# Key copies of the even blocks moved behind the second mask, and half of the first two conversions of v moved from GpSimd to ScalarE

## The chip, the cores and the metric

The kernel runs on one core of one Trainium2 chip. The metric is the time of one execution on the device in microseconds (us). "TensorE", "VectorE", "ScalarE" and "GpSimd" are PE, DVE, ACT and POOL in the profile; SP issues the transfers.

The unchanged kernel scatters: 44 executions of it in this study ran from 184.82 to 189.39 us, with a median of 186.8. A run counts as slow when it is over 1.5% above the fastest run of the same kernel, and the verdicts leave such runs out. No separate slow state of the core is visible here; the scatter is a band, and its causes are part of this story.

## The reference, cut to what matters

Attention over 8 batches, 8 heads, 576 positions and a head size of 64, followed by a gated layer on the joined heads:

```python
mask_plain = (rel >= 0) & (rel < 32)                        # heads 0 to 3
mask_dil = (rel >= 0) & (rel < 128) & (rel % 4 == 0)        # heads 4 to 7
attn = softmax(where(mask, scale * q @ k.T, -1e9));  x = attn @ v
gate = sigmoid(causal depthwise convolution of x over 5 positions, conv_w)
out = (gate * (x @ w_val)) @ w_out
```

## The kernel before

The work is cut into 32 steps, two heads each; four steps make a batch: two plain pairs, then two dilated pairs. I number steps from 0, so steps 2 and 3 are the first dilated ones. Two pairs of one kind in one batch form a group (group 0 plain, group 1 dilated, group 2 plain of the next batch, and so on). Each step does the scores of its own pair on TensorE, the exponentials on ScalarE, the masks on VectorE, the product with v on TensorE, and the transposes of the keys and queries that the next group needs. For plain heads a second copy of the keys is made, kE, in which the even blocks of 96 keys stand next to the keys that a window reaches into. It is copied from kT by VectorE, where the transposes are read out:

```python
else:                                   # the keys of a plain group
    t["kT"] = kTs[(g // 2) % NKT]
    nc.scalar.copy(                     # ScalarE: transposed keys from PSUM to kT
        out=t["kT"][:, z0:z1, 0:RM].rearrange("p z (t r) -> p z t r", r=DIL),
        in_=src.rearrange("p z (r t) -> p z t r", r=DIL))
    ke = t["kE"] = kEs[(g // 2) % NKT]
    kt = t["kT"][:, z0:z1, :].rearrange("p z (u s) -> p z u s", u=NB // 2)
    nc.vector.tensor_copy(ke[:, z0:z1, :, 0:96], kt[:, :, :, 0:96])
    nc.vector.tensor_copy(
        ke[:, z0:z1, 1:NB // 2, 96:128], kt[:, :, 0:NB // 2 - 1, 160:192])
```

The order of a step from number 7 on (earlier steps have a form of their own, marked by `i < EARLY`):

```python
scores(i, 0); scores(i, 1)
run_conv(i - 1)
apply_mask(i, 0)
after_x(i - 1)                                     # reads out xT
if g + 1 < 2 * B:
    trans_main(g + 1, "k" if a == 0 else "q")      # holds the code above
apply_mask(i, 1)
...
attn_v(i, 0); attn_v(i, 1)
normalize(i)
if (a == 0 or i == EARLY) and g + 1 < 2 * B:
    trans_rest(g + 1)                              # the last 64 positions
...                                                # output and value products
```

v of the plain heads comes in as float32 and is converted by four copies on GpSimd, the last two of which the change concerns:

```python
nc.gpsimd.tensor_copy(x[32:64, :, 2:NB, :], w[64:96, :, 0:NB - 2, :])
nc.gpsimd.tensor_copy(x[0:48], w[0:48])
nc.gpsimd.tensor_copy(x[64:96], w[32:64])
nc.gpsimd.tensor_copy(x[96:128], w[64:96])
```

Of the kernel before, what the change touches and what calls it, by code (L numbers as in the profile page):

```python
# [23 lines left out]
def kernel(  # L24
# [11 lines left out]
    nc = tc.nc  # L36

    B, H, S, D = q.shape
# [10 lines left out]
    NB = 6  # L49
# [32 lines left out]
    NKT = 2  # L82
    kTs = [consts.tile([128, 2, S], BF16, name=f"kT{i}") for i in range(NKT)]

    kEs = [consts.tile([128, 2, NB // 2, 128], BF16, name=f"kE{i}") for i in range(NKT)]
    NET = 2
    ets = [consts.tile([128, 2, 2 * HB + 96], BF16, name=f"et{i}") for i in range(NET)]
    NVP = 2
    vPst = [consts.tile([96, 4, NB // 2, 2 * D], FP32, name=f"vPst{i}") for i in range(NVP)]
    vPs = [consts.tile([128, 4, NB, 66], BF16, name=f"vP{i}") for i in range(NVP)]  # L90
# [21 lines left out]
    def bank_b():  # L112
        return bank().bitcast(BF16).rearrange("p (z n) -> p z n", z=2)


    grp_tiles = {}
# [68 lines left out]
    def prep_v(i):  # L185
        b, c, dil, g, a = pair_info(i)
        t = grp_tiles[g]
        e = a + 2
        if not dil:


            w = vPst[b % NVP][:, a:e].rearrange("p h u (j d) -> p h (u j) d", j=2)
            x = vPs[b % NVP][:, a:e, :, 0:D]
            nc.gpsimd.tensor_copy(x[32:64, :, 2:NB, :], w[64:96, :, 0:NB - 2, :])
            nc.gpsimd.tensor_copy(x[0:48], w[0:48])  # L195
            nc.gpsimd.tensor_copy(x[64:96], w[32:64])  # L196
            nc.gpsimd.tensor_copy(x[96:128], w[64:96])  # L197
        else:
            nc.gpsimd.tensor_copy(
                vAs[b % NVD][:, a:e, :, 0:D],  # L200
                t["vst"][:, a:e, :].rearrange("p h (r d) -> p h r d", r=DIL))
            nc.gpsimd.tensor_copy(
                vBs[b % NVD][:, a:e, :, 0:D], t["vBst"][:, a:e, :, :])

    def pair_info(i):
        b, c = i // NCH, i % NCH
        dil = int(c >= NCH // 2)
        return b, c, dil, 2 * b + dil, (c % 2) * 2

    def load_pair(g, a):  # L210
# [26 lines left out]
        out=ident, in_=ident, compare_op=ALU.not_equal, fill=1.0,  # L237
# [5 lines left out]
        out=ident5, in_=ident5, compare_op=ALU.not_equal, fill=1.0,  # L243
# [28 lines left out]
    for j in range(2):  # L272
        for (z, dst) in ((0, mask_p[:, 2 + j, :]), (1, mtmp)):
            band(dst.rearrange("p (r t) -> p r t", r=4), [[1, 4], [4, 24]], 160 * z - j, 2)
        nc.gpsimd.tensor_tensor(
            out=mask_p[:, 2 + j, :], in0=mask_p[:, 2 + j, :], in1=mtmp, op=ALU.add)
# [3 lines left out]
        out=mh, in_=mh, compare_op=ALU.is_ge, fill=1.0,  # L280
# [74 lines left out]
    def trans_main(g, name, pairs=(0, 1)):  # L355

        dil = g % 2
        t = grp_tiles[g]
        ps = bank_b()
        for z in pairs:  # L360
            for m in range(4):
                if not dil and g < 6:
                    for h in range(2):
                        nc.tensor.transpose(
                            out=ps[D * h:D * h + D, z, TM * m:TM * m + TM],
                            in_=hi_bf16(t[name][:, 2 * z + h, D * m:D * m + D]), identity=ident)
                    continue
                elif not dil:
                    src = t[name + "b"][:, m, 2 * z:2 * z + 2, :]
                else:  # L370
                    src = hi_bf16(t[name][:, 2 * z + m // 2, 128 * (m % 2):128 * (m % 2) + 128])
                nc.tensor.transpose(out=ps[:, z, TM * m:TM * m + TM], in_=src, identity=ident)  # L372
        z0, z1 = pairs[0], pairs[-1] + 1
        src = ps[:, z0:z1, :]
        rt = src.rearrange("p z (r t) -> p z r t", r=DIL)
        if not dil:
            if name == "q":
                if "qT" not in t:
                    t["qT"] = qt_pool.tile([128, 2, DIL, T], BF16, name="qT")
                dst = t["qT"][:, z0:z1, :, 0:TM]  # L380
                if g == 0 and z0 == 0:
                    nc.vector.tensor_copy(dst, rt)
                else:
                    nc.scalar.copy(out=dst, in_=rt)
            else:
                t["kT"] = kTs[(g // 2) % NKT]
                nc.scalar.copy(  # L387
                    out=t["kT"][:, z0:z1, 0:RM].rearrange("p z (t r) -> p z t r", r=DIL),
                    in_=src.rearrange("p z (r t) -> p z t r", r=DIL))
                ke = t["kE"] = kEs[(g // 2) % NKT]  # L390
                kt = t["kT"][:, z0:z1, :].rearrange("p z (u s) -> p z u s", u=NB // 2)
                nc.vector.tensor_copy(ke[:, z0:z1, :, 0:96], kt[:, :, :, 0:96])
                nc.vector.tensor_copy(
                    ke[:, z0:z1, 1:NB // 2, 96:128], kt[:, :, 0:NB // 2 - 1, 160:192])
        else:
            A = name + "A"
            if A not in t:
                t[A] = qt_pool.tile([128, 2, RM], BF16, name=A)
            nc.scalar.copy(out=t[A][:, z0:z1, :], in_=src)
            if name == "k":  # L400
                if "kB" not in t:
                    t["kB"] = qt_pool.tile([128, 4, 64, 2], BF16, name="kB")
                nc.scalar.copy(  # L403
                    out=t["kB"][:, 2 * z0:2 * z1, 0:TM - TB, :],
                    in_=src.rearrange("p z (h w t) -> p (z h) t w", h=2, w=2)[:, :, TB:TM, :])

    def trans_rest(g):
        dil = g % 2
# [260 lines left out]
    def warm(n):  # L669
        for _ in range(n):  # L670
            nc.tensor.matmul(out=bank(), lhsT=junk[:, 0:128], rhs=junk, start=True, stop=True)
# [11 lines left out]

    def early_rest(i):

        if i == 0:
            setup_conv_w()
            make_conv_diag(0)
            warm(3)
        run_conv(i - 1)  # L690
        apply_mask(i, 0)
        if i == 0:
            make_conv_diag(1)
        if i > 0:
            after_x(i - 1)
        apply_mask(i, 1)
        if i == 0:
            make_conv_diag(2)
            next_pair(i, ("k",))
        elif i < NCH:  # L700
            next_pair(i)
        if i < NCH:
            warm(2)
        else:
            run_val()
        attn_v(i, 0)
        attn_v(i, 1)
        if i == 0:
            next_pair(i, ("q",))
        normalize(i)  # L710
        if i == 0:
            make_conv_diag(3)
        if i < NCH:
            warm(1)
        else:
            run_val()
            next_pair(i)
        if i == 5:
            run_val()
            run_val()  # L720
        elif i == 6:
            run_out()
            trans_main(4, "k")
            run_out()
# [10 lines left out]
    for i in range(NP):  # L735
        b, c, dil, g, a = pair_info(i)

        if i == 0:
            load_weight(0, moe_w_val)
            load_pair(2, 0)  # L740
        elif i == 1:
            load_pair(2, 2)
        elif i == 2:
            load_weight(1, moe_w_out)
            load_pair(3, 0)
        elif i == 3:
            load_pair(3, 2)
            load_group(4)
        if c % 2 == 0 and 5 <= g + 3 < 2 * B:
            load_group(g + 3)  # L750

        if i == 0:
            prep_v(0)
            make_mask_d()
            prep_v(1)
            make_perm()
        elif i < 3:
            prep_v(i + 1)
        elif i == 3:
            cast_val()  # L760
            prep_v(4)
            swap_val()
        elif i == 4:
            prep_v(5)
            cast_out()
            prep_v(6)
        elif i == 5:
            prep_v(7)
        elif i == 6:
            for m in range(NCH):  # L770
                for h in range(2):
                    swap_out(h, m)
        elif i > 6:
            if i < NP - 1:
                prep_v(i + 1)
            if g + 2 < 2 * B and g % 2 == 0:
                cast(g + 2, "k" if a == 0 else "q")
        scores(i, 0)
        scores(i, 1)
        if i < EARLY:  # L780
            early_rest(i)
            continue
        run_conv(i - 1)
        apply_mask(i, 0)
        after_x(i - 1)
        if g + 1 < 2 * B:
            trans_main(g + 1, "k" if a == 0 else "q")
        apply_mask(i, 1)
        if c == 0 and outs:
            run_out()  # L790
        elif vals:
            run_val()
        attn_v(i, 0)
        attn_v(i, 1)
        normalize(i)
        if (a == 0 or i == EARLY) and g + 1 < 2 * B:
            trans_rest(g + 1)
        if c == 0 and vals:
            run_val()
        for _ in range((2 if len(outs) > 2 else 1) - (c == 0 and i > NCH)):  # L800
            if outs:
                run_out()
        if vals:
            run_val()
# [39 lines left out]
```

## Time and profile before

| | before |
|---|---|
| three timings before the prediction | 186.5, 188.51, 189.39 us |
| span of the profiled execution | 186.8 us |
| TensorE busy | 160.9 us |
| VectorE, ScalarE, GpSimd busy | 133.7, 114.1, 102.6 us |

The page's first part (busy time, share of the span, instructions) and the row of GpSimd in its second part (busy tenths in 40 slices of 4.67 us):

```profile
PE 160.9 (86%) x2850; PEld 107.9 (58%) x2875; DVE 133.7 (72%) x320; ACT 114.1 (61%) x215; POOL 102.6 (55%) x177
POOL 7789949999999758902892268508963000000000
```

TensorE is the engine that is fullest, so the kernel is shortened by taking away its pauses. GpSimd is near full from about 10 to 60 us and takes turns afterwards. While it works, the same VectorE instruction can take longer: the second of the two key copies takes 0.17 us in step 10 of this profile and 0.82 us in step 7, where GpSimd converts v beside it. The prediction quotes the waits and the timeline on which it rests.

### The profile page before, as it was taken

How to read it: one execution, taken by the hardware profiler on the slowest of the kernel's cores; microseconds unless marked ns; L12 is line 12 of the kernel's file. 1: busy time of each engine (PE TensorE's matmuls, PEld its weight loads, DVE VectorE, ACT ScalarE, POOL GpSimd, SP SyncE). 2: the span in 40 equal slices, each digit the busy share in tenths (PEclk: the TensorE clock that was granted, in tenths of full speed). 3: DMA queues.
4: the chain of work that ended last, by engine and by line, in shares of the span. 5: the costliest groups of instructions: out<-in, count | busy, mean ns of one | idle time of the engine just before them, and what ended most of it. 6: DMA issues, size and time to landing. Idle time of an engine off the chain costs nothing.

```text
span 186.8 us, 6930 instructions
## 1 busy us (share of the span) xinstructions
PE 160.9 (86%) x2850; PEld 107.9 (58%) x2875; DVE 133.7 (72%) x320; ACT 114.1 (61%) x215; POOL 102.6 (55%) x177
## 2 busy tenths in 40 slices
PE   6785898788899699989999799979997899999990
PEld 2343565465567476756676466656675667665540
DVE  5594899777769687968876787877696877784320
ACT  3324663646886677776777477657867587654441
POOL 7789949999999758902892268508963000000000
PEclk9879699999999999999999999999999999999998
DMA  5999999999999995959889888879487122222355
GB/s 143 245 299 344 261 233 341 304 273 308 334 270 329 361 228 171 334 164 278 199 278 282 240 232 263 263 243 306 130 261 241 54 65 60 61 57 77 97 168 168
DMA packets 48298, 41.88 MB, mean 224 GB/s; under 512 B 6789, under 2 KB 42629, under 8 KB 48266
## 3 DMA queue, kind: packets, MB, share of 16 engines
q1 hardware_dynamic: 47712, 41.10, 78.3%
q8 instruction: 22, 0.36, 0.9%
q10 hardware_dynamic: 554, 0.34, 0.6%
q14 instruction: 10, 0.08, 0.2%
HBM read 31.99 MB, written 9.44 MB: 222 GB/s over the span
## 4 chain that ended last, share of the span: by engine, by line
PE 55%; DVE 21%; ACT 9%; POOL 6%; issue 4%; DMA 3%; SPq 1%; POOLq 0%; ACTq 0%
PE ps_bank L629 15%; PE ps_bank L612 12%; DVE et L479 9%; PE ps_bank L595 8%; PE ps_bank L372 3%; PE ps_sc L500 3%; DMA vPst<-in_v_dram 3%; ACT kT L387 3%; ACT et L470 3%; PE ps_sc L514 3%; DVE xT L564 3%; PE ps_sc L450 3%; PE ps_sc L467 2%; DVE xn L530 2%; DVE xn L537 2%
## 5 line engine op out<-in xcount | busy, mean ns | idle before, releaser
L470 ACT ACTIVATE et<-ps_sc 128x576 bf16<-128x576 f32 x64 | 38.2, 648 | 18.0 <-PE ps_sc L450 9.5
L634 ACT ACTIVATE osb<-ps_bank 128x512 f32<-128x512 f32 x36 | 21.9, 609 | 34.1 <-PE ps_bank L629 27.5
L618 DVE SCALAR_TENSOR_TENSOR y<-gate,ps_bank 128x288 bf16<-128x288 bf16 x64 | 28.2, 448 | 9.6 <-PE ps_bank L612 8.1
L595 PE MATMUL ps_bank<-xT,conv_diag 64*64 64x288 bf16 (+1 forms) x768 | 27.9, 270 | 0.0
L530 DVE TENSOR_TENSOR xn<-ps_sc,rec 128x768 bf16<-128x768 f32 (+1 forms) x27 | 25.8, 956 | 0.9
L479 DVE TENSOR_TENSOR et<-et,mask_d 128x576 bf16<-128x576 bf16 x32 | 20.9, 653 | 5.1 <-ACT et L470 4.9
L604 ACT ACTIVATE gate<-ps_bank 128x288 bf16<-128x288 f32 x64 | 23.1, 423 | 2.1 <-PE ps_bank L595 2.0
L479 DVE TENSOR_TENSOR et<-et,mask_p 128x576 bf16<-128x576 bf16 x32 | 19.3, 605 | 4.0 <-ACT et L470 4.0
L612 PE MATMUL ps_bank<-xT,w_val_s 128*128 128x288 bf16 x128 | 20.6, 286 | 0.6 <-ACT kB L403 0.6
L595 PEld LDWEIGHTS <-conv_diag 64*64 64x64 bf16 x768 | 19.2, 107 | 3.0 <-DVE qB L432 1.0
L612 PE MATMUL ps_bank<-xT,w_val_b 128*128 128x288 bf16 x128 | 20.1, 286 | 0.4 <-DVE xT L564 0.4
L181 POOL CAST k_b<-k_nat 128x512 bf16<-128x512 f32 x10 | 6.2, 643 | 24.9 <-DMA k_nat<-in_k_dram 16.8
L629 PEld LDWEIGHTS <-y 128*128 128x128 bf16 x144 | 12.6, 97 | 11.7 <-DVE y L618 0.9
L629 PE MATMUL ps_bank<-w_out_b,y 128*128 128x512 bf16 x59 | 17.8, 379 | 0.7
L629 PE MATMUL ps_bank<-w_out_s,y 128*128 128x512 bf16 x60 | 17.7, 380 | 0.6
L564 DVE COPY xT<-ps_bank 128x576 bf16<-128x576 bf16 x32 | 14.5, 454 | 4.1 <-PE ps_bank L562 1.9
L514 PEld LDWEIGHTS <-et 128*128 128x128 bf16 x192 | 8.8, 98 | 13.5 <-DVE et L479 11.0
L514 PE MATMUL ps_sc<-vA,et 128*128 128x65 bf16 x112 | 8.2, 196 | 9.1 <-DVE et L479 9.1
L612 PEld LDWEIGHTS <-w_val_s 128*128 128x128 bf16 x128 | 12.0, 97 | 5.9 <-issue 0.7
L195 POOL CAST vP<-vPst 48x768 bf16<-48x768 f32 x16 | 14.3, 896 | 1.0
L196 POOL CAST vP<-vPst 32x768 bf16<-32x768 f32 x16 | 14.1, 883 | 1.0
L197 POOL CAST vP<-vPst 32x768 bf16<-32x768 f32 x16 | 14.1, 880 | 0.7
(107 smaller groups left out, 302.8 us busy)
## 6 DMA issues: line engine op xcount, KB each, us to landing
k_nat<-in_k_dram SPq DMA_DIRECT2D x12, 512.0 KB, 5.0
q_nat<-in_q_dram SPq DMA_DIRECT2D x12, 512.0 KB, 6.3
vPst<-in_v_dram SPq DMA_DIRECT2D x6, 576.0 KB, 7.3
v_st<-in_v_dram SPq DMA_DIRECT2D x6, 512.0 KB, 6.4
k_nat<-in_k_dram SPq DMA_DIRECT2D x8, 256.0 KB, 6.9
out_dram<-osb SPq DMA_DIRECT2D x8, 256.0 KB, 5.3
q_nat<-in_q_dram SPq DMA_DIRECT2D x7, 256.0 KB, 5.3
out_dram<-osb SPq DMA_DIRECT2D x8, 224.0 KB, 3.9
```

The costliest lines, as they stand in the source:

```text
L195: nc.gpsimd.tensor_copy(x[0:48], w[0:48])
L470: nc.scalar.activation(out=e3, in_=ps[:, :, 0:HB], func=AF.Exp, scale=scale)
L479: nc.vector.tensor_tensor(out=e3, in0=e3, in1=m, op=ALU.mult)
L514: nc.tensor.matmul(out=ps[hf][:, x * AVS:x * AVS + D + 1], lhsT=et[:, hf, col:col + 128], rhs=rhs, start=True, stop=True)
L530: nc.vector.tensor_tensor(out=dst, in0=av[:, :, :, 0:D], in1=rec[0:R, :, :, None].to_broadcast([R, 2, 6, D]), op=ALU.mult)
L564: nc.vector.tensor_copy(xTs[b % NXT][:, c, :, 2:], pr)
L595: nc.tensor.matmul(out=pss[G][D * hp:D * hp + D, o * T:(o + n) * T], lhsT=conv_diag[D * h:D * h + D, c, K - 1 - m, :], rhs=xt[D * h:D * h ...
L604: nc.scalar.activation(out=gate, in_=pss[G][:, 0:HB], func=AF.Tanh, scale=0.5)
L612: nc.tensor.matmul(out=ps[:, 0:HB], lhsT=w[:, mc, c * 128:(c + 1) * 128], rhs=xt[:, mc, 2 * G:2 * G + 2, 2:], start=(mc == 0), stop=(mc == ...
L618: nc.vector.scalar_tensor_tensor(out=y_half[G][:, c, b % YB * HB:(b % YB + 1) * HB], in0=gates.pop((b, c, G)), scalar=1.0, in1=ps[:, 0:HB] ...
L629: nc.tensor.matmul(out=ps, lhsT=y_half[G][:, c, y0:y0 + 128], rhs=w[:, c, :], start=(c == 0), stop=(c == NCH - 1),)
L634: nc.scalar.mul(out=osb, in_=ps, mul=0.5)
```

## The change

The intent has two parts. Part A: the key copies wait for kT, which ScalarE writes, and VectorE works in program order, so they hold up the second mask and with it TensorE (in step 14 before, the copy waits 1.04 us for kT, the mask comes behind it at 83.88 us, and TensorE waits 1.19 us for the mask). They are moved to the end of the step, as their keys are not needed before the next plain group. Part B: in steps 0 and 1 GpSimd is the slowest (busy for 4.41 and 4.68 us of the 5 us from 10 and from 15 us on, ScalarE for 2.30 and 1.26), so two of the four conversions of v go to ScalarE.

```diff
-            nc.gpsimd.tensor_copy(x[64:96], w[32:64])
-            nc.gpsimd.tensor_copy(x[96:128], w[64:96])
+            if b > 0:
+                upper_v(i)
...
+    def upper_v(i):
+        b, c, dil, g, a = pair_info(i)
+        w = vPst[b % NVP][:, a:a + 2].rearrange("p h u (j d) -> p h (u j) d", j=2)
+        x = vPs[b % NVP][:, a:a + 2, :, 0:D]
+        copy = nc.scalar.copy if b == 0 else nc.gpsimd.tensor_copy
+        copy(out=x[64:96], in_=w[32:64])
+        copy(out=x[96:128], in_=w[64:96])
...
-                ke = t["kE"] = kEs[(g // 2) % NKT]
-                kt = t["kT"][:, z0:z1, :].rearrange("p z (u s) -> p z u s", u=NB // 2)
-                nc.vector.tensor_copy(ke[:, z0:z1, :, 0:96], kt[:, :, :, 0:96])
-                nc.vector.tensor_copy(
-                    ke[:, z0:z1, 1:NB // 2, 96:128], kt[:, :, 0:NB // 2 - 1, 160:192])
+                if len(pairs) == 1:
+                    even_keys(g, z0, z1)
...
+    def even_keys(g, z0=0, z1=2):        # the four lines removed above
...
     def early_rest(i):
 
+        if i < 2:
+            upper_v(i)
...
         if (a == 0 or i == EARLY) and g + 1 < 2 * B:
             trans_rest(g + 1)
+            if dil:
+                even_keys(g + 1)
```

The late copies come in steps 10, 14, 18, 22 and 26, and, by `i == EARLY`, in step 7 for group 4, whose keys step 8 needs at once.

> **What bounds the kernel now.** I read the page first. TensorE is busy for 160.9 us of a span of 186.8 us, at full granted clock from about 25 us on. The chain that ended last lies mostly on TensorE, and VectorE holds a fifth of it:
>
> ```profile
> PE 55%; DVE 21%; ACT 9%; POOL 6%; issue 4%; DMA 3%; SPq 1%; POOLq 0%; ACTq 0%
> ```
>
> So TensorE sets the pace, and what can be won is the time in which it stands still: 26 us, spread over the span. I then read the list of waits (engine, line, whom it waited for: us in total, times, longest) to see who makes it stand still.
>
> ```profile
> PE ps_sc L514 <- DVE et L479: 9.1, 13, 1.8
> DVE kE L392 <- ACT kT L387: 9.0, 7, 1.9
> ```
>
> The first line is the largest wait of TensorE's matmuls: the attention-times-v product of the dilated heads waits for the masked scores. The second names a VectorE instruction that idles 9.0 us for ScalarE and has nothing to do with the mask: the copy of the even blocks' keys (kE) from kT, which ScalarE writes. The timeline of step 14 (start us, duration us) joins the two:
>
> ```profile
> 82.05 0.46 DVE L564 COPY xT<-ps_bank 128x576 bf16<-128x576 bf16 x1
> 82.50 1.02 ACT L387 COPY kT<-ps_bank 128x1024 bf16<-128x1024 bf16 x1
> 82.85 0.29 PE L514 MATMUL ps_sc<-vA,et 128*128 128x65 bf16 x4
> 83.55 0.31 DVE L392 COPY kE<-kT 128x576 bf16<-128x576 bf16 x1 [1.04 <-ACT kT L387]
> 83.88 0.45 DVE L479 TENSOR_TENSOR et<-et,mask_d 128x576 bf16<-128x576 bf16 x1
> 84.39 0.30 PE L514 MATMUL ps_sc<-vA,et 128*128 128x65 bf16 x4 [1.19 <-DVE et L479]
> ```
>
> VectorE works in program order. After xT it comes to the key copy, whose kT is ready only at 83.5; the second mask, whose scores were ready long before (both exponentials end by 82.0), stands behind it. TensorE has finished its first half at about 83.2 and waits 1.19 us for that mask. The same picture stands in steps 10, 18, 22 and 26 (every fourth step, the first dilated pair of each batch); read from the timeline of each, TensorE waits 1.32, 1.19, 1.19, 1.19 and 1.84 us for steps 10, 14, 18, 22, 26: 6.73 of the 9.1 us. These keys are not used until two steps later.
>
> The start is bound otherwise. From 8 to 20.8 us the chain runs through GpSimd, which converts v and makes the masks:
>
> ```profile
> 17.42 0.82 POOL L197 CAST vP<-vPst 32x768 bf16<-32x768 f32 x1
> ...
> 18.30 0.79 PE L500 MATMUL ps_bank<-vP,et 64*128 64x65 bf16 x23 [1.58 <-POOL vP L197]
> ...
> 25.64 0.60 POOL L194 CAST vP<-vPst 32x512 bf16<-32x512 f32 x1 [2.65 <-DMA vPst<-in_v_dram]
> 35.06 0.82 POOL L197 CAST vP<-vPst 32x768 bf16<-32x768 f32 x1
> ...
> 37.70 0.39 PE L500 MATMUL ps_sc<-vP,et 64*128 64x65 bf16 x14 [0.45 <-DVE et L479]
> ```
>
> TensorE waits 1.58 us for the last conversion of step 1. But GpSimd's own line has a second origin: at 25.64 it starts again, after 2.65 us of idling, when v of step 4 has landed, and works without a gap to 35.9, where v of step 5 is done. Step 5's product uses it at 36.9 (first half) and 37.7 (second half).
>
> [...]the kT copy takes 585 ns for 512 elements and 1018 ns for 1024, or 0.846 ns per element. [...]the key copies take 0.31 us (576 elements) and 0.19 us where GpSimd is idle (step 14), but 0.31 + 0.82 us at 47.5 us where it is busy, and a mask of step 2 takes 2.52 us beside four conversions of w_val. [...]Part B is a move[...] from a GpSimd that is busy for 4.4 to 4.7 us of each 5 us from 10 to 20 us to a ScalarE that is busy for 1.3 to 2.3.
>
> **The change, part A: keys behind the second mask and the remainders.** No work is added or removed; two VectorE copies move within a step.
>
> In steps 10, 14, 18, 22 and 26 the mask can start when xT ends. In step 14 that is 82.42, so it ends at 82.9, before TensorE has finished the first half (83.2). The whole wait goes: 6.73 us over the five steps. TensorE is the chain before and after these waits, so I count all of it. What comes back: the copies, 0.5 us, now stand after the remainder copies, ahead of the next y and mask. VectorE has a gap there:
>
> ```profile
> 86.13 0.34 DVE L423 COPY qT<-ps_bank 128x64 bf16<-128x64 bf16 x2
> 86.39 0.45 DVE L618 SCALAR_TENSOR_TENSOR y<-gate,ps_bank 128x288 bf16<-128x288 bf16 x1
> 87.18 0.46 DVE L479 TENSOR_TENSOR et<-et,mask_d 128x576 bf16<-128x576 bf16 x1 [0.34 <-ACT et L470]
> ```
>
> 0.34 us of idling before the next mask takes most of the 0.5 us; GpSimd is idle at that point in four of the five steps, so they stay short. I charge 0.1 us per step: +0.5 us.
>
> The diff has one more place, easily overlooked: keys of group 4, transposed at the end of step 6. Before, their copy stood at the head of step 7. There mask 0 was not held up by it, since its exponential ends at 48.5 and the copies end at 48.54; freeing this wins little, 0 to 0.6 us by fewer collisions with GpSimd, say 0.3. Now the copies stand at the end of step 7, and step 8 needs those keys at once:
>
> ```profile
> 51.77 0.23 PE L450 MATMUL ps_sc<-qT,kE 64*64 64x96 bf16 x2
> ...
> 52.24 0.34 DVE L423 COPY qT<-ps_bank 128x64 bf16<-128x64 bf16 x2
> ```
>
> The scores of step 8 begin at 51.77 (their last ones wait for the qT copy) and the convolution follows at 52.78. In the new order the keys come after the qT copies (end about 52.6) and GpSimd is busy there, so the two copies take about 1.0 us (1.03, 1.00 and 1.13 us in the three crowded cases of this trace). The scores begin at about 53.6, take 0.5 us, and the convolution starts at 54.1: a loss of 1.3 us. Net for group 4: +1.0 us.
>
> Part A: -6.7 + 0.5 + 1.0 = -5.2 us.
>
> **Part B: ScalarE converts half of v in steps 0 and 1.** It removes four GpSimd casts (0.93 + 0.99 + 0.82 + 0.82 = 3.6 us)[...]. ScalarE has the room: in step 0 it idles from 8.6 to 10.25 us, in step 1 from 16.3 to 20.0, but there the copies stand in front of kA, kB and qA and push these about 1.1 us later, to about 17.3. Worked forward: step 0's product, behind fewer collisions on VectorE, ends about 0.6 us earlier; step 1's product no longer waits for GpSimd to 18.25 but for ScalarE to about 16.1 (-2.1 us); step 2's scores need qA (17.3) and come at 17.5 instead of 19.56. The mask of step 2 then escapes the w_val casts, which cannot start before w_val lands at 20.5 us. So by step 3 some 2 to 3 us are won.
>
> They are not kept. v of step 4 lands at 25.5 us whatever the engines do, as the DMA engines are full from 5 to 50 us (share above 1.0 in each stretch of 5 us), and up to 35 us the issuing queue waits only for earlier transfers, not for an engine. GpSimd's chain from 25.64 to 35.9 is therefore the same as before, and step 5's product cannot start before 35.95. Its second half then comes at about 36.3 instead of 37.70: at most 1.4 us survive. If the second mask of step 2 still loses the race with the w_val casts (I make it 20.35 us against 20.5), about 0.85 us survive. I take -1.2 us.
>
> **Sum.** -5.2 - 1.2 = -6.4 us; 188.5 - 6.4 = 182.1 us.
>
> **Rivals.**
> Everything of part B is kept (-3 us or more): speaks for it, that GpSimd is the chain to 20.8 us; against it, the landing at 25.5 and the unbroken GpSimd line to 35.9. It would give about 180 us.
> Part A only moves the wait: VectorE is busy 72% of the span, and if the late copies meet GpSimd at each step (1.0 instead of 0.5 us) the next mask comes 0.5 to 0.7 us later and TensorE, which in steps 15, 19 and 23 already waits 0.15 to 0.40 us there, waits that much more. It would take back 2.5 to 3.5 us: about 185 us. Against it: GpSimd is idle at 86, 105 and 126 us.
> ScalarE becomes the bound in the early steps, if its copies from SBUF are slower than estimated or v lands late and holds up kT: part B worth nothing, 183.3 us.
> Group 4's loss is not there, because the copies run short or the scores are late anyhow: 181 us.
> Transfers bind the faster steady state: their share is 0.8 to 1.1 in the middle, but GpSimd's casts of k stand 14 us ahead of their use, so I give this little.
>
> **Range and chances.** The steps of part A repeat five times and were measured each; their uncertainty is 1.5 us. Part B and group 4 carry about 1 us each, and the three timings of the kernel before spread from 186.5 to 189.39. I take 180.4 to 184.8 us as the range for 8 in 10. 2% is 184.7 us. Faster by over 2%: 0.86; within 2%: 0.13; slower: 0.01.
>
> **What would show it.** Right: the wait of the dilated product for the mask falls from 9.1 us to about 2 us and ScalarE's kT no longer stands as releaser of kE in these five steps; in step 14 the second half follows the first without a gap; the distance from the scores of step 14 to those of step 15 falls from 5.7 to about 4.5 us. TensorE shows a new wait of about 1.3 us for kE before the scores of step 8. Step 1's product starts near 16.2, step 5's second half near 36.3 behind GpSimd's last cast of v. Wrong: key copies of 0.8 us or more in the late steps with a longer wait in steps 11, 15, 19; step 5 well before 36 us; scores of step 8 without a wait.

## The result, and the profile after

The changed kernel ran in 178.84 us (median of four runs, 178.26 to 179.49; before in the same rounds 187.5). The ratio is 0.9616, with a 95% interval of 0.9536 to 0.9696: faster. The prediction of 182.1 us had the direction and the class right, and the measured time lies below its range of 180.4 to 184.8. Ratios are the mean time of one kernel's fast runs over that of the other's in the same rounds, so not quite the ratio of the medians that I quote.

In the profile after, lines have moved: the mask is L492 (before L479), the dilated product L527 (L514), the plain product L513 (L500), the plain scores L463 (L450), the key copies L416 and L417 (L392 and L393), kT on ScalarE L395 (L387). The page of the changed kernel, first part and chain:

```profile
PE 159.0 (89%) x2850; PEld 107.5 (60%) x2875; DVE 128.1 (72%) x320; ACT 117.5 (66%) x219; POOL 98.3 (55%) x173
PE 68%; DVE 17%; POOL 5%; ACT 5%; issue 3%; ACTq 0%; DVEq 0%; POOLq 0%
```

The span is 9.0 us shorter (177.8), TensorE does the same work in it, and its share of the chain has gone from 55 to 68%. The list of waits (engine, line, whom it waited for: us in total, times, longest):

```profile
DVE kE L416 <- ACT kT L395: 2.2, 1, 2.2
PE ps_sc L527 <- DVE et L492: 1.6, 5, 0.6
PE ps_sc L463 <- DVE kE L416: 1.1, 1, 1.1
```

The first two are what is left of 9.0 and 9.1 us. The third is new: the scores wait for the late keys of group 4. Step 14 in the timeline of the changed kernel (start, duration), as the counterpart of the one in the prediction:

```profile
80.35 0.45 DVE L492 TENSOR_TENSOR et<-et,mask_d 128x576 bf16<-128x576 bf16 x1
80.77 0.29 PE L527 MATMUL ps_sc<-vA,et 128*128 128x65 bf16 x4
80.96 0.29 PE L527 MATMUL ps_sc<-vA,et 128*128 128x65 bf16 x4
...
82.95 0.30 DVE L416 COPY kE<-kT 128x576 bf16<-128x576 bf16 x1
83.05 1.19 ACT L483 ACTIVATE et<-ps_sc 128x576 bf16<-128x576 f32 x2
83.17 0.19 DVE L417 COPY kE<-kT 128x128 bf16<-128x128 bf16 x1
83.27 0.45 DVE L631 SCALAR_TENSOR_TENSOR y<-gate,ps_bank 128x288 bf16<-128x288 bf16 x1
83.74 0.46 DVE L492 TENSOR_TENSOR et<-et,mask_d 128x576 bf16<-128x576 bf16 x1
```

The mask now precedes the first half of the product, and the second half starts 0.19 us after the first (1.54 us before: 82.85 and 84.39 in the prediction's fence). The key copies end at 83.3, y follows, and the mask comes at 83.74, about when the first half of step 15's exponentials (two in 1.19 us from 83.05) is done. TensorE does not wait for that mask.

Step 8 in the same timeline, at its scores:

```profile
50.03 0.34 DVE L416 COPY kE<-kT 128x576 bf16<-128x576 bf16 x1
50.29 0.85 DVE L417 COPY kE<-kT 128x128 bf16<-128x128 bf16 x1
50.42 0.23 PE L463 MATMUL ps_sc<-qT,kE 64*64 64x96 bf16 x2 [1.06 <-DVE kE L416]
...
51.19 0.23 PE L463 MATMUL ps_sc<-qT,kE 64*64 64x96 bf16 x2 [0.49 <-DVE kE L417]
```

TensorE waits 1.06 and then 0.49 us for these two copies, the second of which takes 0.85 us beside GpSimd's cast of v from 50.26 to 51.08 us, and 0.19 us in step 14, where GpSimd is idle. And the start:

```profile
16.46 0.84 PE L513 MATMUL ps_bank<-vP,et 64*128 64x65 bf16 x23 [0.46 <-DVE qB L445]
...
34.20 0.95 POOL L211 CAST vP<-vPst 32x768 bf16<-32x768 f32 x1
35.21 0.53 PE L513 MATMUL ps_sc<-vP,et 64*128 64x65 bf16 x23 [1.47 <-POOL vP L211]
```

Step 1's product comes at 16.46 instead of 18.30 us, and step 5's waits for GpSimd's last cast of v, as foretold, if at 35.21 us and not at 36.3.

To see where the time went, I measured every step by the start of its first exponential on ScalarE, which is a cleaner mark than the end of a matmul. The sums, in us:

| stretch | before | after | change | prediction |
|---|---|---|---|---|
| start of step 7 | 47.85 | 45.36 | -2.49 | -1.2 |
| steps 7 and 8 (group 4) | 9.26 | 10.67 | +1.41 | +1.0 |
| steps 10, 14, 18, 22, 26 | 31.51 | 24.02 | -7.49 | -6.73 |
| the steps after these | 22.68 | 21.51 | -1.17 | +0.5 |
| all other steps | 53.76 | 54.42 | +0.66 | 0 |
| start of step 31 | 165.06 | 155.98 | -9.08 | -6.4 |

That is one profile of each. As the runs below show, the first two profiles exaggerate: the kernel before had a bad draw in its start, a draw being what one execution happens to get.

### The profile page after: what moved, and what is told of

Read it like the earlier page. It is cut to its first block, busy times and chain, and to the rows that moved or that the text cites. A ratio compares the mean times of both kernels' runs of the same rounds, so it can differ in the third digit from the quotient of the medians.

```text
span 177.8 us, 6929 instructions
## 1 busy us (share of the span) xinstructions
PE 159.0 (89%) x2850; PEld 107.5 (60%) x2875; DVE 128.1 (72%) x320; ACT 117.5 (66%) x219; POOL 98.3 (55%) x173
## 4 chain that ended last, share of the span: by engine, by line
PE 68%; DVE 17%; POOL 5%; ACT 5%; issue 3%; ACTq 0%; DVEq 0%; POOLq 0%
PE ps_bank L642 16%; PE ps_bank L625 14%; PE ps_bank L608 11%; DVE et L492 6%; PE ps_bank L380 5%; PE ps_sc L513 4%; PE ps_sc L480 3%; PE ps_sc L527 3%; PE ps_bank L684 3%; DVE xn L543 3%; PE ps_sc L463 3%; PE ps_bank L562 2%; DVE xT L577 2%; ACT et L483 2%; PE ps_bank L575 2%
## 5 line engine op out<-in xcount | busy, mean ns | idle before, releaser
L492 DVE TENSOR_TENSOR et<-et,mask_d 128x576 bf16<-128x576 bf16 x32 | 17.4, 542 | 7.1 <-ACT et L483 7.0
L492 DVE TENSOR_TENSOR et<-et,mask_p 128x576 bf16<-128x576 bf16 x32 | 19.1, 598 | 4.5 <-ACT et L483 4.5
L194 POOL CAST vP<-vPst 32x512 bf16<-32x512 f32 x16 | 10.0, 626 | 7.3 <-DMA vPst<-in_v_dram 5.2
L513 PEld LDWEIGHTS <-et 64*128 64x128 bf16 x384 | 7.6, 96 | 10.3 <-issue 4.9
L625 PEld LDWEIGHTS <-w_val_b 128*128 128x128 bf16 x128 | 11.5, 98 | 3.7 <-issue 0.2
L542 DVE RECIPROCAL rec<-ps_sc 128x12 f32<-128x12 f32 (+1 forms) x27 | 6.2, 231 | 9.5 <-PE ps_sc L513 8.2
```

The lines of the kernel that those rows point to most:

```text
L492: nc.vector.tensor_tensor(out=e3, in0=e3, in1=m, op=ALU.mult)
L513: nc.tensor.matmul(out=ps[z][:, x * AVS:x * AVS + D + 1], lhsT=et[D * z:D * z + D, h2, col:col + 128], rhs=vPs[b % NVP][D * z:D * z + D, a ...
L625: nc.tensor.matmul(out=ps[:, 0:HB], lhsT=w[:, mc, c * 128:(c + 1) * 128], rhs=xt[:, mc, 2 * G:2 * G + 2, 2:], start=(mc == 0), stop=(mc == ...
```

## The experiments

Sixteen runs were made, in sessions on different chips (11, 9, 10 and 5; that of the first result is not on record), so across sessions the ratios compare better than the medians. The theory to begin with: part A removes the waits of five steps, group 4 pays some of it back, part B gains what GpSimd's line up to step 5 allows. The rivals: the late copies cost time in the following steps; the drop in the start is not part B but a race in the kernel before; the place of the copies matters and not the wait for kT.

### Each part alone

keys_only is the changed kernel with all of v on GpSimd:

```diff
-            if b > 0:
-                upper_v(i)
+            upper_v(i)
...
-        copy = nc.scalar.copy if b == 0 else nc.gpsimd.tensor_copy
+        copy = nc.gpsimd.tensor_copy
...
-        if i < 2:
-            upper_v(i)
```

> Part A alone: the key copies moved as in the change, all of v converted on GpSimd as before. Theory (the two parts bind in different stretches, so their gains add): the five steps 10, 14, 18, 22, 26 become shorter by 1.36 us each, or 1.5 to 1.9 in steps 10 and 26, as in the changed kernel (7.5 us in all); group 4's new wait before the scores of step 8 costs 1.2 to 1.6 us; the steps right after the five become shorter by about 1 us in all; so 6 to 7.3 us under the kernel before, a ratio of 0.961 to 0.968. Rival (the gain of the changed kernel in the middle exists only because the start was moved against the transfers): 4 us or less, a ratio above 0.978.

Measured: 181.09 us (median of 4; ratio 0.9628, 0.9512 to 0.9744), with the kernel before at 187.46 in the same rounds. The five steps took 24.58 us, steps 7 and 8 10.63. So part A, group 4 included, is worth some 6.4 us.

v_only keeps the key copies in the old place:

```diff
-                if len(pairs) == 1:
-                    even_keys(g, z0, z1)
+                even_keys(g, z0, z1)
...
-            if dil:
-                even_keys(g + 1)
```

> Part B alone: ScalarE converts half of v in steps 0 and 1, keys where they were before. Theory (GpSimd's line from the landing of v of step 4 to v of step 5 caps the gain): step 5's product ends about 2.4 us earlier, at 35.8 us, and this is kept to the end since group 4's keys are not moved: ratio 0.985 to 0.990. My forecast had 1.2 us, 0.9936. Rival (the gain of the start is given back in the middle to collisions or transfers): ratio 0.995 or more, with the steps from 9 on longer than before.

Measured: 185.68 us (ratio 0.9924, 0.9849 to 0.9999): 1.8 us by the medians and under the 2% mark. It lies between the theory (0.985 to 0.990) and the rival (0.995 or more), and the interval holds both. Its step 7 starts at 44.58, 3.3 us ahead of the first profile of before, but step 10 took 7.75 us (6.43 in that profile). There the earlier time brings the key copies beside GpSimd's casts (0.82 us each, from 59.87 to 61.55); the timeline of v_only (the mask is L491 here, the product L526, the second copy L416):

```profile
60.79 0.82 DVE L416 COPY kE<-kT 128x128 bf16<-128x128 bf16 x1
...
62.02 0.30 PE L526 MATMUL ps_sc<-vA,et 128*128 128x65 bf16 x4 [1.92 <-DVE et L491]
```

The second copy takes 0.82 instead of 0.17 us, and TensorE waits 1.92 us where it had waited 1.32. Behind that wait its granted clock was moreover at 0.50 from 63.1 to 66.5 us, which probably lengthens the step too (in after_again, below, 24 convolution matmuls took 1.41 us at 0.50 and 0.79 at 1.00). So in this profile the earlier start made the wait longer that part A removes. That the two parts are worth more together than apart is not shown by the times: they gained 6.4 and 1.8 us apart, and together 8.7 us in the first result and 7.1 over all runs.

### Group 4's keys in their old place

keys4_early is the changed kernel, but step 7 makes its key copies where the kernel before made them:

```diff
-                if len(pairs) == 1:
+                if len(pairs) == 1 or g == 4:
...
-            if dil:
+            if dil and i != EARLY:
                 even_keys(g + 1)
```

> The changed kernel, but with the keys of group 4 copied where they were before (ahead of step 7's masks). Theory: that copy was free there, as VectorE waits 2.9 us for ScalarE's exponential at the head of step 7, and it is the whole cause of the new wait of 1.06 + 0.49 us before step 8's scores. So the wait goes, step 7 falls from 6.1 us to about 4.6, and the kernel is 1.1 to 1.5 us faster than the changed one: about 177.5 us, ratio to before 0.953 to 0.957 if the changed kernel is at 0.9616. Rival (the scores of step 8 are late anyhow, waiting for the remainders' copies at 50.1 us, so the loss is only moved): gain under 0.4 us.

Measured: 177.65 us (ratio 0.9511, 0.944 to 0.9582). Step 7 took 3.92 us (6.12 in the changed kernel), and the scores of step 8 no longer wait for keys. Step 11 gave 0.7 us back (4.94 against 4.23 us): with 2.3 us less before it, its copies and masks fall beside GpSimd's casts (the second copy takes 0.85 us beside a cast at 62.86, the first mask 0.84 beside one at 63.73; in the changed kernel 0.17 and 0.45).

### w_val behind the conversion of v

In the changed kernel GpSimd converts half of w_val ahead of v of step 5. wval_late turns that order:

```diff
         # step 3
             prep_v(4)
-            swap_val()
         # step 4
             prep_v(5)
+            swap_val()
             cast_out()
```

> The changed kernel, but GpSimd converts v of step 5 before it swaps the halves of w_val. Theory (the cap of the start is GpSimd's work between v of step 4 and v of step 5, not the transfers themselves): v of step 5 lands at about 29 us and is converted by 32.6 instead of 35.2; step 5's product no longer waits 1.47 us for GpSimd, and 1.0 to 1.5 us are won, ratio to before 0.953 to 0.957 if the changed kernel is at 0.9616. Rival (the landing of v of step 5 or the swapped weights bind next): a new wait for w_val_s in step 5's second products or for v in step 6, and a gain under 0.4 us.

Measured: 178.27 us (ratio 0.9536, 0.9467 to 0.9605). Step 5 took 5.72 instead of 6.88 us, and in the trace step 5's product no longer waits for GpSimd. So GpSimd's line to v of step 5 was the cap on part B, as the prediction said. By the medians it gains 0.6 us on the first result of the changed kernel and 1.4 on all runs of it, which is within what the changed kernel scatters.

Both edits together, in `both`:

> The changed kernel with both mends: keys of group 4 at their old place, and v of step 5 converted ahead of the swap of w_val. Theory (they act at 51 and at 35 us, so they add): 1.0 us for the first and 0.6 to 1.2 us for the second, so 176.5 to 177.3 us, ratio to before 0.943 to 0.950. Rival (step 5's earlier product runs into the next conversion, and the two share one gain): 177.6 us or more.

Measured: 177.37 us (ratio 0.9492, 0.943 to 0.9553). It isn't distinguishable from keys4_early alone: step 2 (4.98 us) and step 11 (5.21 us) came out long in its profile.

### Are the late copies free?

keys_double issues the late copies of the five steps twice:

```diff
             if dil:
                 even_keys(g + 1)
+                if i != EARLY:
+                    even_keys(g + 1)
```

> The changed kernel with each late key copy issued twice (same result) in steps 10, 14, 18, 22 and 26: 0.5 us more VectorE work at the very place where the change put it. My forecast charged 0.1 us per step for one copy there. Theory (VectorE waits for ScalarE's exponential there, and what is later than that is caught up before TensorE needs the second mask): doubling costs 0 to 0.2 us per step, under 1 us in all, so within 0.5% of the changed kernel; the steps 11, 15, 19, 23 keep 4.2 to 4.6 us. Rival (VectorE's work is on the path there): 0.5 us per step, 2.5 us in all, 1.4%.

Measured: 180.68 us, ratio 0.9685 (0.9602 to 0.9768), by itself unclear: 1.8 us above the first result of the changed kernel, though in its profile the five steps (24.59 us) and the steps after them (21.50) were as in the changed kernel. So I ran it again beside the changed kernel on one chip.

> The changed kernel, timed again beside the next one on one chip. Theory: 178.3 to 179.3 us as before, with a spread of little over 1 us, since its first dilated mask comes about 2 us ahead of the conversions of w_val and is not in the race any more.

> The doubled late key copies once more, now beside the changed kernel. Its steps in the profile were within 0.2 us of the changed kernel's (156.15 against 155.98 us at step 31), but its times were 179.6 to 182.25 us, 1.9 us over the changed kernel's of another session. Theory (the copies are hidden, the difference was the session or other steps): within 0.6 us of the changed kernel's median here. Rival (the copies are on the path in most runs and the profiled run was a lucky one): 1.5 to 2.5 us over it.

Measured: after_again 180.44 us (178.73 to 181.6), keys_double_again 178.84 (178.1 to 180.12). The kernel with twice the copies is the faster one here, though after_again's profile has a slow stretch of its own (below). The steps say more: with twice the copies the five steps took 24.60 and 24.16 us in the two profiles and the steps after them 21.50 and 21.54, against 24.33 and 21.82 in the mean of four profiles of the changed kernel. So the copies are hidden. The timeline of keys_double_again at the end of step 14, from the second pair of copies on:

```profile
82.07 0.31 DVE L416 COPY kE<-kT 128x576 bf16<-128x576 bf16 x1
82.30 0.19 DVE L417 COPY kE<-kT 128x128 bf16<-128x128 bf16 x1
...
82.77 0.45 DVE L492 TENSOR_TENSOR et<-et,mask_d 128x576 bf16<-128x576 bf16 x1
```

With the second pair the mask comes later behind its exponential than with one, but TensorE has other work until it needs it, and step 15 takes 4.23 us, as with one pair. But the expectation for after_again failed: the unchanged repeat was 1.6 us above its first result. That became the open question below.

### The wait or the place?

keys_stale gives a wrong result on purpose. It is the kernel before, with the copies in the old place, but in the five steps, and for group 4 too, they read the other of the two kT buffers, which was finished long ago:

```diff
+                src_kT = kTs[(g // 2 + 1) % NKT] if len(pairs) == 2 else t["kT"]
-                kt = t["kT"][:, z0:z1, :].rearrange("p z (u s) -> p z u s", u=NB // 2)
+                kt = src_kT[:, z0:z1, :].rearrange("p z (u s) -> p z u s", u=NB // 2)
```

> Wrong result on purpose: the kernel before, keys copied at their old place ahead of the second mask, but from the other kT buffer, which was filled four steps earlier: the wait for ScalarE goes, the 0.5 us of copying stays in front of the mask. Theory (the wait is most of the loss, the place a smaller part): in step 14 the mask ends at about 83.4 less the shift instead of 82.9, so TensorE still stands about 0.38 us; the step takes about 4.7 us (5.67 before, 4.31 after), and the five steps together lose 5 to 6 us of the 7.5. Rival (it is the place in the order alone that counts[...]): less than 3 us. Total: 4.5 to 6.5 us under before.

Measured: 182.38 us, ratio 0.9729 (0.9654 to 0.9803), unclear against the 2% mark. The five steps took 26.67 us, 4.84 less than in the first profile of before, while the changed kernel has 7.49 less. Its timeline in step 14 (product L515, mask L480):

```profile
82.42 0.45 DVE L480 TENSOR_TENSOR et<-et,mask_d 128x576 bf16<-128x576 bf16 x1
82.53 0.29 PE L515 MATMUL ps_sc<-vA,et 128*128 128x65 bf16 x4
...
82.93 0.30 PE L515 MATMUL ps_sc<-vA,et 128*128 128x65 bf16 x4
```

Without the wait the second half still comes 0.40 us after the first (0.19 in the changed kernel), because the copies stand ahead of the mask. So the wait for kT carries about two thirds of the gain, and the place the rest. Step by step the shares differ: in steps 14, 18 and 22, where the copies are short (0.30 and 0.19 us), the wait carries 1.14 of 1.36 us. In step 10 they fall beside GpSimd's casts and take 0.55 and 0.85 us, and without the wait only 0.30 of 1.51 us are won.

### The kernel before, three more times

> The kernel before, unchanged, profiled once more. In the first profile the first dilated mask (step 2) came at 20.78 us, just after GpSimd had begun the four conversions of w_val, and took 2.52 us; in the run with the keys alone, whose program is the same up to there, it came at 20.43 us, ahead of them, took 0.83 us, and step 7 began at 46.66 instead of 47.85 us. Theory (that is a race which goes either way from run to run, so about 1.2 us of the changed kernel's lead in the profile is the first profile's bad luck): step 7 begins anywhere between 46.5 and 48 us, and it goes with the length of that mask. Rival (the two programs differ systematically): step 7 at 47.8 us again, mask 2.5 us.

> The kernel before, a third profile. In the second one, by chance, the first dilated mask came at 20.41 us and took 0.83 us, step 7 began at 45.66 us and the run took 185.59 us; in the first the mask took 2.52 us, step 7 began at 47.85, and the run took 188.56. Theory (a race at 20.4 to 21 us between that mask and the four conversions of w_val decides between two starts): long mask with step 7 near 47.8 and a time near 188 to 189, or short mask with step 7 near 45.7 to 46.7 and 185.5 to 186.5. Rival (the start varies for other reasons): the length of the mask and the time do not go together.

> The kernel before, a fourth profile, for the same question: long first dilated mask with a time of 188 us or more, or short mask with 186.5 us or less.

Measured: 185.59, 184.98 and 186.41 us (single runs, so their state is unknown), and in their profiles step 7 starts at 45.66, 45.17 and 44.95 us instead of 47.85. The changed kernel's first profile has 45.36. So the -2.49 us of the table was the draw, in good part. What was drawn is seen in step 2. The timeline of the first profile of before:

```profile
20.71 2.28 POOL L336 CAST w_val_b<-w_st 128x512 bf16<-128x512 f32 x4
20.78 2.52 DVE L479 TENSOR_TENSOR et<-et,mask_d 128x576 bf16<-128x576 bf16 x1 [0.21 <-POOL vB L202]
```

and of before_again:

```profile
20.41 0.83 DVE L479 TENSOR_TENSOR et<-et,mask_d 128x576 bf16<-128x576 bf16 x1
21.19 2.51 POOL L336 CAST w_val_b<-w_st 128x512 bf16<-128x512 f32 x4 [0.26 <-DMA w_st<-in_moe_w_val_dram]
```

In the first profile the mask came 0.07 us behind the first of four successive casts and took 2.52 us; in the other three it was ahead and took 0.83 or 0.84. To be ahead is not enough, though. keys_stale has the same program up to there (its mask is L480):

```profile
20.84 3.06 DVE L480 TENSOR_TENSOR et<-et,mask_d 128x576 bf16<-128x576 bf16 x1
21.29 2.29 POOL L336 CAST w_val_b<-w_st 128x512 bf16<-128x512 f32 x4
```

Here the mask began 0.45 us ahead of the four casts and still ended behind the last of them. What the two long cases share is that GpSimd went on without a break: its first cast of w_val starts 0.35 and 0.34 us after the cast of vB before it, in the three short cases 0.41 to 0.66 us. Whether such a break lets the mask through was not tested. The half clock may have made the mask late in the first profile; that was not tested either. The windows of the first profile of before (window, its length; busy time and count of PE, PEld, DVE, ACT and POOL; granted clock; DMA share; GB/s):

```profile
17.00:18.00 1.00, 0.00 (x0) 0.00 (x0) 0.00 (x0) 0.00 (x0) 0.94 (x2) 1.00 1.05 393
18.00:19.00 1.00, 0.70 (x23) 0.63 (x22) 0.00 (x0) 0.00 (x0) 0.87 (x5) 0.68 1.06 381
19.00:20.00 1.00, 1.00 (x17) 0.55 (x13) 0.84 (x3) 0.00 (x0) 1.00 (x3) 0.50 1.10 342
```

TensorE stood still for GpSimd's conversion of v, and then ran at half clock from 18.4 to 21.8 us; in the other three profiles it was at full speed from 17.6 us on at the latest. (The traces of before_again and before_third hold no clock record before 17.55 and 17.12 us, and the windows print 1.00 there. It was probably half: with TensorE busy throughout, they hold 8 and 9 matmuls from 15.0 to 15.5 us; keys_only and keys_only_4early, at a recorded 0.50, hold 9 each from 14.5 to 15.0, and the first profile, at a recorded 1.00, holds 13. The mean clock listed for such a run would then be too high.) The profiles of keys_only and keys_only_4early had half clock around 20 us too and started step 7 at 46.66 and 45.73 us without the long mask, so the clock may do harm by itself; two profiles don't show it. The good starts of the kernel before have their price in step 10, which took 7.03, 7.03 and 8.36 us (6.43 in the first profile), apparently for the reason seen in v_only: while TensorE stands still there, GpSimd is busy for 0.44 to 0.50 us of each half us. In before_fourth, the longest, TensorE's granted clock was moreover 0.50 for about 3.4 us from 63.5 us on, right behind the wait of 1.94 us that ended at 62.99.

### What separates 178.8 from 180.4

after_again had a step 8 of 5.84 us where the first profile had 4.55. The windows of after_again, with the same columns:

```profile
50.00:51.00 1.00, 0.40 (x16) 0.27 (x20) 0.82 (x2) 0.00 (x0) 0.94 (x2) 0.86 1.09 349
51.00:52.00 1.00, 1.00 (x34) 0.89 (x37) 0.10 (x1) 0.78 (x2) 0.94 (x2) 0.50 1.13 319
```

In the first profile of the changed kernel the window from 51 to 52 us has 1.00. In after_again the granted clock fell to 0.50 from about 50.7 to 54.1 us, directly behind TensorE's stop for group 4's keys, and the same 24 convolution matmuls took 1.41 instead of 0.79 us. keys_double had the same drop (step 8: 5.92 us), keys_double_again had not (4.55). So I suspected that the stop costs 1.4 us, and now and then 1.3 us more by the clock. Four runs were to test it. keys4_early_again is keys4_early unchanged; after_third and after_fourth are the changed kernel; keys_only_4early is keys_only with the edit of keys4_early.

> Theory: the stop of TensorE in step 7/8 for group 4's keys costs 1.4 us by itself and now and then a further 1.3 us by the drop of the granted clock behind it. Without the stop: steps 7 and 8 together 8.6 to 8.9 us (changed kernel 10.67 and 11.92 in its two profiles), granted clock 1.00 from 45 to 56 us, median 177.0 to 178.3 us, and a ratio to the kernel before of 0.945 to 0.955. Rival (the drop comes from elsewhere, and the first result of 177.65 was a lucky session): the clock falls in steps 7 to 9 here too, the median is 179 us or more.

Measured: 178.02 us (177.83 to 178.77; ratio 0.9557, 0.9512 to 0.9602). Steps 7 and 8 took 8.88 us and the clock stayed at 1.00 there.

> Part A's five late copies alone, v on GpSimd as before and group 4's keys in the old place. Theory: the five steps take 24.0 to 24.7 us (kernel before 31.5 to 32.8 in four profiles), steps 7 and 8 8.6 to 9.2, and the start is as in the kernel before, with its draw of step 2. Median 178.5 to 180.0 us, that is 1 to 2 us above keys4_early_again, which is then part B's worth. Rival (part B is worth nothing against a good draw): median within 0.5 us of keys4_early_again.

Measured: 179.04 us (ratio 0.9591, 0.9542 to 0.964). Five steps 24.17 us, steps 7 and 8 9.13. Part B is thus worth 1.0 us by the medians of these two kernels, though the two intervals overlap.

> The changed kernel, unchanged. Theory: either step 8 takes about 4.55 us with the clock at 1.00 from 50 to 55 us and the run takes 178 to 179.5 us, or about 5.85 us with the clock at 0.50 for some 3.4 us and the run takes 179.5 to 181.5 us. Rival: the time varies by over 1 us between runs whose step 8 is alike.

> As after_third: a run with step 8 at about 4.55 us and a full clock should take 178 to 179.5 us, one with step 8 at about 5.85 us and the clock at 0.50 for 3.4 us 179.5 to 181.5 us.

Measured: after_third 179.2 us and after_fourth 180.13 us, both with a step 8 of 4.55 us and no drop of the clock there. after_third agrees; after_fourth misses its bound by 0.6 us. It loses 0.46 us on after_third in step 7 and 0.18 and 0.30 us in steps 10 and 11, so that it is 1.1 us behind by step 22. So the drop of the clock is one cause of the scatter and not the only one.

The traces tell more about when the clock falls. Its records, but for a run's last, last 3.41 us or a multiple of it (3.41, 6.83 and 163.84 us in the first profile of before, 3.41, 10.24 and 157.01 in that of the changed kernel), so they lie on a grid that starts anew in each run (the first record starts at 4.71 us in the one and at 5.98 in the other). In the piece of the grid that ended at the drop, TensorE was busy for 1.62 us (after_again, 47.30 to 50.72; its longest waits there were 1.06 and 0.63 us) and 1.74 us (keys_double, 46.94 to 50.35); before the drops in step 10, for 1.49 us (v_only) and 1.47 us (before_fourth). In the six profiles that kept full clock through the stop, the grid cuts it otherwise, and the least busy piece has 1.70 to 2.3 us. So it seems to matter where the stop falls on the grid. But 1.70 us without a drop and 1.74 us with one give no clean threshold (in before_third even 1.57 us, from 140.0 on, brought none), and no run tests this.

All twelve runs of the changed kernel have a median of 179.7 us (178.26 to 181.6); all ten of keys4_early have 177.9 (177.23 to 178.77). The version without the stop is the faster one and scatters by 1.5 instead of 3.3 us. It beats both kernels of the case.

## Why the prediction was right or wrong

The mechanism was right in its main parts, and the sizes were not. Two steps of the sum failed most: the base, 188.5 us where 44 runs have 186.8, and the wait in the five steps, 6.73 us where the steps became shorter by 7.8. With the right base alone the forecast would have been 180.4 us, the lower end of its range. With four profiles of each kernel the terms can be read with less of the luck of one draw (means of the four, us):

| term | prediction | measured |
|---|---|---|
| five steps without the wait | -6.73 | 32.11 to 24.33: -7.8 |
| late copies in the steps after | +0.5 | 22.02 to 21.82: -0.2 |
| group 4 | +1.0 | 9.13 to 10.86: +1.7 |
| part B, to the start of step 7 | -1.2 | 45.91 to 45.34: -0.6 |
| other steps | 0 | 53.73 to 54.00: +0.3 |

Step 31 starts at 162.88 us before and 156.35 after, in the mean: 6.5 us earlier, and the prediction's sum was 6.4. That agreement is luck, because the errors cancel: 1.8 us more were won in the five steps and behind them, and 1.6 less at group 4, in part B and in the other steps.

**The five steps: right in kind, undersized by 1.1 us.** The prediction summed TensorE's waits. Two things are missing in that. First, the profile counts a wait from the end of the matmul before it (in step 14 from 83.20 to 84.39 us), and matmuls overlap: in step 14 the distance from the first half to the second fell from 1.54 to 0.19 us, so 1.35 were won where the wait read 1.19. In the trace the matmuls of a half start 29 to 40 ns apart and last 191 to 204 ns each, so about 0.16 us of each are hidden when another matmul follows. The 0.16 us of difference have that size; but the profile models where a matmul ends, so this is a consistency and no test. By the lengths of the steps, 0.17 to 0.19 us more were won than the wait had read in steps 10, 14, 18 and 22 (in step 14, 1.36 us where 1.19 were read), and 0.06 us in step 26. The start-to-start distance was the measure to take. Secondly, the first profile's step 10 was the mildest of four: in the other three the copies met GpSimd (busy for 0.44 to 0.50 us of each half us there; in the first it was done at 64.44 us, before the second copy at 64.53) and the step took 0.6 to 1.9 us longer, nearly all of which part A removes (4.92 to 5.43 us after).

**The late copies: the charge of 0.1 us per step was wrong.** They end about when the next exponential is ready, TensorE needs the mask later still, and even doubled they showed no loss. In the first pair of profiles the following steps even gained 1.17 us; in the mean of four it is 0.2, so I don't count it as an effect. The rival "part A only moves the wait" falls.

**Group 4: found in advance, and undersized by 0.7 us.** The stop is there as predicted, by 1.06 and 0.49 us. The size lacked two things: step 7 gives VectorE an idle stretch that nobody uses (2.9 us before a mask at 46 us), so its early place was free, and behind the stop the granted clock fell to 0.50 in 2 of 8 profiles. The kernels without the stop confirm the term: 179.7 against 177.9 us.

**Part B: the step was right, and the profile of before misled about its size.** The cap by GpSimd's line is shown by wval_late: with v of step 5 converted earlier, step 5's product no longer waits for GpSimd. What the prediction had wrong is how far the kernel before stays from this cap. It read step 5's second half at 37.7 us and the last cast of v at 35.9, so 1.4 us could be won. That holds in the first profile alone. In before_again, before_third and before_fourth step 5's product already waits for that cast, for 1.47, 0.48 and 0.48 us, and the cast ends at 35.46, 34.85 and 34.63 us; in the changed kernel's four it ends at 34.91 to 35.25. A good start of the kernel before is at the cap already, and part B can't shorten it. Over all nine profiles with part B and GpSimd's order unchanged, step 7 starts at 44.6 to 45.5 us, 45.1 in the mean; over the seven without part B at 45.0 to 47.9, 46.2 in the mean. So the worth is 1.1 us on average over these draws, close to the 1.2 predicted by luck (the table's 0.6 rests on four and four). The clock goes along with it. Of the seven without part B, the four with half clock somewhere between 18 and 23 us start step 7 at 45.7 to 47.9, the three with full clock there at 45.0 to 45.7. Of the nine with part B, five had half clock there and start at 44.9 to 45.4, four had not and start at 44.6 to 45.5. So part B seems to make the start insensitive to what is lost around 20 us, since step 5 waits for GpSimd anyway; that the clock is what costs the others their time is not shown. That the mask of step 2 would escape w_val's casts was right (it came at 18.99 us, the casts at 20.67), and the four conversions on ScalarE, whose length was the author's estimate, took 0.83 us each.

**The base: 1.7 us too high.** The prediction started from 188.5, the median of three runs; 44 runs have 186.8. The prediction noted the spread of the three and still centred on their median. This is the prediction's largest single error.

Together, by medians: base 188.5 to 186.8 is 1.7 us; the change, -6.4 predicted and -7.1 measured (186.8 to 179.7), is 0.7; and the four runs first measured lay 0.9 below the median of twelve. That makes the 3.3 us from 182.1 to 178.84. The centre of all runs, 179.7, is still below the range, so the miss is real: a base from too few runs makes up half of it, and the wait read too short points the same way. What stays open: why the changed kernel still scatters by about 1 us between runs with the same step 8, how often the clock falls behind group 4's stop (2 of the 8 profiles that have it), and why the runs show 0.6 us more of a change (7.1) than the four profiles (6.5).

## What to carry to other kernels

When an engine works in program order, ask of every instruction whose input comes late what stands behind it, and move it to a place where that engine waits anyway; but check the first use of its result, since one of six moved pairs here was needed at once and cost 1.8 us. Read what a wait is worth from start to start of the work around it, and take the baseline from more than three runs before you subtract from it. Add up the measured terms before you trust a sum that came out right, since errors can cancel. Where a few tenths of a microsecond decide how long one engine waits for another, one profile is one draw: look at several before you explain a start.
